# Thresholded attention and a mixer on one core: scores in four quadrants, the up product in 512 columns, quarter-tile down products, the first batch ahead

## The chip, the core and the metric

The kernel runs on one core of a Trainium2 chip. The metric is the device time of one execution in microseconds (us), the median of several runs. The engines are TensorE (PE; its weight loads are listed apart as PEld), VectorE (DVE), ScalarE (ACT), GpSimd (POOL) and SyncE (SP). Each works through its own instructions in the order in which they were written, and waits for other engines by semaphores. DMA is started from SP and POOL here (at the very start from ACT too) and runs on 16 DMA engines that all queues share.

## The reference

There are 8 batches, 8 heads, 576 positions and heads of 64. Attention keeps only the scores within `tau` of a row's maximum; its result, as a 576 x 512 matrix per batch, goes through a mixer of rank 32 along the positions and a hidden layer of 2048.

```python
def _attn_ref(q, k, v, tau) -> np.ndarray:
    scale = 1.0 / np.sqrt(q.shape[-1])
    scores = scale * np.matmul(q, k.transpose(0, 1, 3, 2))
    thresh = np.max(scores, axis=-1, keepdims=True) - tau
    scores = np.where(scores >= thresh, scores, -1000000000.0)
    ...
    attn = np.exp(scores)
    attn = attn / (np.sum(attn, axis=-1, keepdims=True) + 1e-09)
    return np.matmul(attn, v).astype(np.float32)
...
def _moe_ref(x, U, V, w_ch1, w_ch2) -> np.ndarray:
    xt = x.transpose(0, 2, 1)
    h = xt @ U @ V
    u = x + h.transpose(0, 2, 1)
    ch = np.maximum(u @ w_ch1, 0.0) @ w_ch2
    return (u + ch).astype(np.float32)
```

Inputs and output are float32.

## The kernel before

**Tiles.** Heads are taken in pairs: 32 pairs, four per batch. A pair's 576 positions are four tiles of 128 rows and a rest of 64; the rests of two neighbouring pairs share one tile, "tile 4". So two pairs have nine tiles, and the whole kernel 144 score steps, one per tile and pair of heads.

**Attention, per pair.** Twelve DMAs bring q, k and v (`load_tasks`, L268 to L306; the four of v are issued by POOL at L304 and L305). PE transposes q and k in float32 (L334, L349), ACT copies them into `qkT`. A score step (L401 to L414) is a float32 product with a contraction of 64: each head has half of the array's rows, and one matmul makes 128 score rows in 288 columns (L406, four matmuls per step, "two row halves"). Tile 4 uses quadrants of 64 x 64, since its two halves come from two pairs (L411, eight matmuls). In the trace a float32 matmul is two records. Per step and head DVE then scales and takes the row minimum of the negated scores (L427), ACT takes the exponential (L451), and DVE selects and sums (L459) into `w_ring`, a ring of eight bfloat16 tiles. POOL copies the last 64 columns of such a tile a second time (L484), which makes 640. It is then transposed into `wT`: by a DMA transpose from SP (L471; L475 for tile 4), or, for one head of the first eight pairs (`x == 1 and p < EARLY`, 32 tiles), by five PE transposes (L480) and an ACT copy (L494). Values are split into a high and a low bfloat16 part (ACT L371, L372; POOL L376 to L379), and the value product AV (L527, 18 matmuls of 288 columns in "two column halves") runs over both. Its result is transposed back (L554, L557), scaled (L570, L574) and narrowed.

**Mixer.** The rank-32 step is two small PE groups (L592, L607), for tile 4 one more matmul of 512 columns per batch (L610). The sum u is narrowed and transposed (L640, L644 for tile 4) into `uT`, 576 columns per batch. The up product (L682) covers these columns in two halves of 288: 2 x 16 tasks per batch of four matmuls, each followed by a relu on ACT (L692). The down product (L708) makes one tile of 128 rows in two halves of eight matmuls of 512 columns, and holds one PSUM bank for both. Tile 4 holds 64 rows of an even and 64 of the next odd batch. DVE adds u (L721), POOL issues two stores per tile (L734, L735, L738). PSUM has four banks for all of this beside four for the scores.

**The weights** come by POOL's DMAs (L750 to L752, L756 with four casts L759 to L762, eight pieces of W1 at L766, eight of W2 at L769). Each waits in `gate` for the first L427 of a score step.

**The order** is made while the program is built. Every piece is a `Task` with an engine, a cost, a due offset `off` and what it depends on; `Order.run` (L73 to L145) plays them with these costs, and takes on each engine the task that is ready first or, within a small patience, has the lowest rank. Mixer products have a due step (`when`), ahead of which they only fill gaps. Where PE would be idle for over 0.45 us by this plan, it puts in filler matmuls (L234) that compute nothing. The plan's times are not the chip's; only the order that comes of it stays.

## Time and profile before

| | |
|---|---|
| median of 3 runs | 664.34 us (664.3 to 664.85) |
| profiled execution, device time | 662.74 us |
| its span, first to last instruction | 660.9 us |
| mean granted TensorE clock | 0.995 |
| PE busy | 629.7 us (95%) |
| DVE, ACT, POOL busy | 516.4, 492.8, 477.9 us |
| memory read and written | 37.90 and 9.44 MB |

In a group's row stand line, engine, operation, output <- input, shape and count; then busy time, the mean of one in ns, and the engine's idle time ahead of it with what ended it. In rows in order of time stand the start, the duration, and the count of merged records. Matmul records overlap, so what a matmul costs is the distance to the next start and not its duration. Some matmul records are missing (534 of 576 in one group).

### The profile page before, as it was taken

To read this page: it belongs to the slowest core of one execution; us is meant where nothing else is said; L and a number is where in the kernel's file an instruction comes from. 1 tells how busy PE (TensorE), PEld (TensorE's weight loads), DVE (VectorE), ACT (ScalarE), POOL (GpSimd) and SP (SyncE) were. 2 spreads that over 40 slices of the span, in tenths; PEclk is the share of its full clock that TensorE was granted. 3 is DMA by queue.
4 is the path that set the end of the run, shared out by engine and by line. 5 is a ranking of instruction groups with operands and counts; after the bars stand their busy time and mean duration, and the time that the engine had idled before them with its cause. 6 is when DMAs were issued, how large, how long until landed. Compare 5 with 4: busy or idle time off the path is not lost.

```text
span 660.9 us, 15748 instructions
## 1 busy us (share of the span) xinstructions
PE 629.7 (95%) x5121; PEld 409.6 (62%) x5171; DVE 516.4 (78%) x1370; ACT 492.8 (75%) x1122; POOL 477.9 (72%) x864
## 2 busy tenths in 40 slices
PE   8999889999999999999999999999999999999994
PEld 4566556666566666666666666666666666567652
DVE  5999799698798898797997798888995898973001
ACT  4888799888587886778777787868787777776430
POOL 9989788998997779948794889778696965430111
PEclk9999899999999999999999999999999999999998
DMA  4776989999878889869784998976799957561112
GB/s 102 128 112 116 160 121 166 138 153 183 171 152 122 148 148 168 160 101 149 146 159 74 167 170 145 163 130 128 139 184 116 182 122 138 88 108 22 40 41 48
DMA packets 199890, 86.13 MB, mean 130 GB/s; under 512 B 184320, under 2 KB 190416, under 8 KB 199808
## 3 DMA queue, kind: packets, MB, share of 16 engines
q1 hardware_dynamic: 175280, 42.22, 47.1%
q0 software_dynamic: 23648, 42.69, 30.4%
q8 instruction: 41, 0.67, 0.4%
q14 instruction: 41, 0.34, 0.2%
q10 hardware_dynamic: 880, 0.21, 0.1%
HBM read 37.90 MB, written 9.44 MB: 72 GB/s over the span
## 4 chain that ended last, share of the span: by engine, by line
PE 66%; ACT 4%; DVE 3%; issue 2%; POOL 1%; DMA 0%; POOLq 0%; DVEq 0%; ACTq 0%
PE bank L708 18%; PE bank L682 15%; PE scores L406 14%; PE bank L527 9%; PE bank L334 2%; ACT e_sb L451 2%; PE bank L554 2%; PE scores L411 2%; PE bank L592 1%; PE bank L640 1%; ACT R L692 1%; PE bank L607 1%; DVE w_ring L459 1%; DVE s_sb L427 1%; DMA vraw<-in_v_dram 0%
## 5 line engine op out<-in xcount | busy, mean ns | idle before, releaser
L427 DVE TENSOR_SCALAR_CACHE_REDUCE s_sb<-scores 128x576 f32<-128x576 f32 x288 | 206.3, 752 | 63.8 <-PE scores L406 55.2
L451 ACT ACTIVATE e_sb<-s_sb,m 128x576 bf16<-128x576 f32 x288 | 220.4, 768 | 45.4 <-DVE s_sb L427 44.2
L459 DVE SCALAR_TENSOR_TENSOR w_ring<-s_sb,thr,e_sb 128x576 bf16<-128x576 f32 x288 | 232.6, 840 | 6.5 <-issue 4.1
L484 POOL COPY w_ring<-w_ring 128x64 bf16<-128x64 bf16 x288 | 113.4, 407 | 76.3 <-DVE w_ring L459 71.9
L406 PE MATMUL scores<-qkT 64*128 64x288 f32 x1024 | 167.9, 430 | 0.3
L682 PE MATMUL bank<-uT,W1b 128*128 128x288 bf16 x1024 | 138.9, 286 | 2.2 <-ACT R L692 0.9
L708 PE MATMUL bank<-W2b,R 128*128 128x512 bf16 x534 | 129.0, 379 | 4.2 <-issue 1.1
L682 PEld LDWEIGHTS <-W1b 128*128 128x128 bf16 x1024 | 96.1, 98 | 47.2 <-issue 21.5
L692 ACT ACTIVATE R<-bank 128x288 bf16<-128x288 f32 x256 | 94.4, 406 | 40.6 <-PE bank L682 35.7
L406 PEld LDWEIGHTS scores<-qkT 64*128 64x128 f32 x1024 | 95.0, 186 | 43.3 <-issue 11.5
L708 PEld LDWEIGHTS <-R 128*128 128x128 bf16 x576 | 54.5, 98 | 63.9 <-issue 8.5
L288 POOL DMA_DIRECT2D qkraw<-in_q_dram x125 | 82.3, 664 | 16.2 <-PE bank L349 12.3
L288 POOL DMA_DIRECT2D vraw<-in_v_dram x128 | 86.1, 677 | 4.6 <-issue 2.8
L288 POOL DMA_DIRECT2D qkraw<-in_k_dram x125 | 81.5, 657 | 3.2 <-issue 2.4
L527 PE MATMUL bank<-wT,vh 128*64 128x288 bf16 x1152 | 80.4, 290 | 1.6 <-ACT R L692 1.2
L527 PEld LDWEIGHTS <-vh 128*64 128x64 bf16 x1152 | 63.1, 110 | 17.8 <-issue 11.4
L721 DVE TENSOR_TENSOR o<-bank,x 128x512 f32<-128x512 f32 x36 | 24.7, 686 | 45.7 <-PE bank L708 40.3
L734 POOL DMA_DIRECT2D out_dram<-o x32 | 17.9, 561 | 57.1 <-DVE o L721 56.4
L439 ACT ACTIVATE thr<-m,tau_t 128x2 f32<-128x2 f32 x144 | 40.7, 283 | 5.2 <-DVE s_sb L427 5.2
L342 ACT COPY qkT<-bank 128x512 f32<-128x512 f32 x64 | 35.9, 582 | 10.6 <-PE bank L334 10.4
L334 PE MATMUL bank<-ident,qkraw 128*128 128x128 f32 x256 | 37.3, 279 | 4.5 <-DMA qkraw<-in_q_dram 2.6
L377 POOL TENSOR_TENSOR vh<-vraw,vh 128x512 bf16<-128x512 f32 x32 | 38.9, 1216 | 3.5 <-ACT vh L371 0.6
(74 smaller groups left out, 604.8 us busy)
## 6 DMA issues: line engine op xcount, KB each, us to landing
vraw<-in_v_dram POOLq DMA_DIRECT2D x128, 80.0 KB, 3.6
out_dram<-o POOLq DMA_DIRECT2D x72, 128.0 KB, 3.4
qkraw<-in_k_dram POOLq DMA_DIRECT2D x63, 80.0 KB, 4.0
qkraw<-in_q_dram POOLq DMA_DIRECT2D x62, 80.0 KB, 3.7
wT<-w_ring SPq DMA_TRANSPOSE x288, 4.0
qkraw<-in_q_dram POOLq DMA_DIRECT2D x63, 64.0 KB, 3.7
qkraw<-in_k_dram POOLq DMA_DIRECT2D x62, 64.0 KB, 3.6
W1b<-in_moe_w_ch_dram POOLq DMA_DIRECT2D x8, 256.0 KB, 4.7
```

What stands on the lines that cost most here:

```text
L288: queue.dma_start(raw[part, to, j, :], src[:, of, j, :])
L334: nc.tensor.transpose(bank[t.got[0]][:, i * P:(i + 1) * P], pr.qkraw[:, t0 + i, :, :], ident)
L406: nc.tensor.matmul(pair_bank[j][:, c, 0:HC], pr.tT[hs, 0, i * P:(i + 1) * P], pr.tT[hs, 1, c * HC:(c + 1) * HC], start=True, stop=True)
L427: nc.vector.tensor_scalar(out=s_sb.rearrange("p (a c) -> p a c", a=2), in0=pair_bank[x][:, :, 0:HC], scalar1=-scale, scalar2=None, op0=ALU ...
L439: nc.scalar.activation(out=st["thr"], in_=st["m"], func=ACT.Identity, bias=tau_t[:, 0:1], scale=1.0)
L451: nc.scalar.activation(out=st["e", x], in_=st["s", x], func=ACT.Exp, bias=st["m"][:, x:x + 1], scale=-1.0)
L459: nc.vector.scalar_tensor_tensor(out=w_sb[:, 0:S], in0=st["s", x], scalar=st["thr"][:, x:x + 1], in1=st["e", x], op0=ALU.is_le, op1=ALU.mu ...
L484: nc.gpsimd.tensor_copy(out=w_sb[:, S:640], in_=w_sb[:, 512:S])
L527: nc.tensor.matmul(av[64 * j:64 * j + 64, 0:HC], pr.vh[:, kt, part, j, :] if kt < 4 else pr.vh4[:, j, :], pr.wT[:, kt, j, c * HC:(c + 1) * ...
L682: nc.tensor.matmul(bank[t.got[0]][:, 0:HC], W1b[:, dt, ft * P:(ft + 1) * P], bt.uT[:, dt, c * HC:(c + 1) * HC], start=(dt == 0), stop=(dt ...
L692: nc.scalar.activation(out=R2[:, ft, lo:lo + HC], in_=bank[t.got[0]][:, 0:HC], func=ACT.Relu)
L708: nc.tensor.matmul(ch, R2[:, ft, lo:lo + P], W2b[:, ft, :], start=(ft == 0), stop=(ft == 15))
```

## The change

1. *Scores.* Every step uses quadrants: a tile's 128 rows are two halves of 64, so a step is eight matmuls of 64 x 288 where it was four of 128 x 288. The plan's allowance for a change of array mode (`SWITCH`) becomes one per mode.
2. *Up product.* `uT` holds a batch's 512 columns of tiles 0 to 3; one matmul covers 512 columns, 16 tasks per batch and one relu each. Tile 4's 128 columns, of two batches together, get a tile `uT4` of their own, and four tasks per two batches (four hidden tiles of 128 columns side by side in a bank, one relu for the four). Their chain (rank-32 matmul, sum, cast, transposes, copy) is taken out of the last pair's tasks and becomes tasks of its own, at the odd batch.
3. *Down product.* Four tasks of four matmuls per tile, where it was two of eight. Tile 4 comes last.
4. *First batch ahead.* All tasks of pairs 0 to 3 get `off` lower by 20. The loads of v for these pairs (16) are issued by SP. The weights' `off` falls from 25 to 5, V's load and casts are two tasks, and the small ones come first.
5. *Transposes of w.* PE now does 17 tiles: those of `x == 1`, pairs below 8, tiles 2 and 3, and both of pair 3's tile 3. SP's DMA transposes do 15 more.
6. *The plan's DMA times* are kept per queue, with a shared part. Due steps of the mixer move from `18 * (b + 1) + 8` to `+ 12`.

```diff
-    SWITCH = 0.093
-    PARTS = {"S": "two row halves", "S4": "quadrants", "AV": "two column halves"}
+    SWITCH = {"quadrants": 0.145, "two column halves": 0.11, None: 0.095}
+    PARTS = {"S": "quadrants", "AV": "two column halves"}
...
-                if self.PARTS.get(t.kind) != self.PARTS.get(kind):
-                    s += self.SWITCH
+                parts = self.PARTS.get(t.kind)
+                if parts != self.PARTS.get(kind):
+                    s += self.SWITCH[parts]
...
+                q = e != POOL
+                begin = max(moved[q], at[e] + 0.6)
+                shared = min(t.dma, max(0.0, moved[1 - q] - begin))
+                moved[q] = begin + t.dma + shared
+                moved[1 - q] += shared
+                t.end = moved[q] + 1.2
...
-            return add(e, 0.7, fn, deps, dma=0.4, off=20.0 if p else -9.0)
+            return add(e, 0.7, fn, deps, dma=0.2 if e == POOL else 0.35, off=20.0 if p else -9.0)
...
-            loads["v"].append(one("v", POOL, lo, slice(1, 6), slice(0, 5), j, freed))
-            loads["v"].append(one("v", POOL, hi, slice(0, 5), slice(4, 9), j, freed))
+            ev = SP if p < NPAIR else POOL
+            loads["v"].append(one("v", ev, lo, slice(1, 6), slice(0, 5), j, freed))
+            loads["v"].append(one("v", ev, hi, slice(0, 5), slice(4, 9), j, freed))
...
+        now = -20.0 if p < NPAIR else 0.0
         def scores(_):
             for c in range(2):
+                cs = slice(c * HC, (c + 1) * HC)
                 for j in range(2):
                     hs = slice(64 * j, 64 * j + 64)
-                    if i < 4:
-                        nc.tensor.matmul(pair_bank[j][:, c, 0:HC],
-                                         pr.tT[hs, 0, i * P:(i + 1) * P],
-                                         pr.tT[hs, 1, c * HC:(c + 1) * HC], start=True, stop=True)
-                        continue
-                    for a in two:
-                        nc.tensor.matmul(pair_bank[j][a.part4, c, 0:HC], a.tT[hs, 0, 512:S],
-                                         a.tT[hs, 1, c * HC:(c + 1) * HC], start=True, stop=True)
+                    for h in range(2):
+                        a, rows, part = pr, slice(i * P + HB * h, i * P + HB * h + HB), \
+                            slice(HB * h, HB * h + HB)
+                        if i == 4:
+                            a, rows, part = two[h], slice(512, S), two[h].part4
+                        nc.tensor.matmul(pair_bank[j][part, c, 0:HC], a.tT[hs, 0, rows],
+                                         a.tT[hs, 1, cs], start=True, stop=True)
...
-        S_ = done["S", p, i] = add(PE, 0.97, scores, deps, off=-6.0, kind="S" if i < 4 else "S4")
+        S_ = done["S", p, i] = add(PE, 0.97, scores, deps, off=now - 6.0, kind="S", steps=1)
...
-            if x == 1 and p < EARLY and i < 4:
-                t = done["wT", tiles[0]] = add(PE, 0.28, turn_pe, [dup] + free, off=-1.0, banks=1,
+            if i < 4 and (x == 1 and p < EARLY and i >= 2 or p == NPAIR - 1 and i == 3):
+                t = done["wT", tiles[0]] = add(PE, 0.28, turn_pe, [dup] + free, off=now - 1.0, banks=1,
...
+        h = done["h", p] = add(PE, 0.23, spread, [tt, weights0[1]], off=now - 3.0, banks=1, kind="h")
...
+                bt.uT = upool.tile([P, 4, 512], BF16, name="uT", tag="uT")
+            nc.scalar.copy(out=bt.uT[:, pr.hp, :], in_=bank[uT_.got[0]][:, 0:256].bitcast(BF16))
+        done["uT", p] = add(SCA, 0.53, copy_u, [uT_, got("uT", p - 1)], off=now - 2.0, frees=[uT_])
...
+        if not last:
+            return
+        def spread4(t):
+            nc.tensor.matmul(bank[t.got[0]], Vb[:, 512:640], bt.tt, start=True, stop=True)
+        h4 = done["h4", pr.b] = add(PE, 0.22, spread4,
+                                    [done["tt", p - n] for n in range(4)] + [weights0[1]], off=-1.0,
+                                    banks=1, kind="h")
+        def sum_u4(_):
+            nc.vector.tensor_add(out=bt.x4[bt.h4, :], in0=bank[h4.got[0]][bt.h4, :],
+                                 in1=bt.x4[bt.h4, :])
+        u4 = done["u4", pr.b] = add(VEC, 0.62, sum_u4, [h4] + [done["xb", p - n] for n in range(4)],
+                                    off=1.0, frees=[h4])
+        if not bt.odd:
+            return
+        def narrow_u4(_):
+            nc.scalar.copy(out=ub4, in_=bt.x4)
+        ub4_ = add(SCA, 0.57, narrow_u4, [u4, done["u4", pr.b - 1], got("uT4_", pr.b - 2)], off=1.0)
+        def turn4(t):
+            ps = bank[t.got[0]][:, 0:256].bitcast(BF16)
+            for dt in range(4):
+                nc.tensor.transpose(ps[:, dt * P:(dt + 1) * P], ub4[:, dt * P:(dt + 1) * P], identb)
+        uT4_ = done["uT4_", pr.b] = add(PE, 0.23, turn4, [ub4_] + done.get(("p1r", pr.b - 4), []),
+                                        off=-1.0, banks=1, kind="uT")
+        def copy_u4(_):
+            bt.uT4 = upool.tile([P, 4, P], BF16, name="uT4", tag="uT4")
+            nc.scalar.copy(out=bt.uT4, in_=bank[uT4_.got[0]][:, 0:256].bitcast(BF16).rearrange(
+                "p (t c) -> p t c", t=4))
+        done["uT4", pr.b] = add(SCA, 0.53, copy_u4, [uT4_], off=0.0, frees=[uT4_])
...
-        due = 18 * (b + 1) + 8
+        due = 18 * (b + 1) + 12
...
-            for ft in range(16):
-                def up(t, ft=ft, c=c):
-                    for dt in range(4):
-                        nc.tensor.matmul(bank[t.got[0]][:, 0:HC], W1b[:, dt, ft * P:(ft + 1) * P],
-                                         bt.uT[:, dt, c * HC:(c + 1) * HC],
-                                         start=(dt == 0), stop=(dt == 3))
-                t = add(PE, 0.49, up, uT + weights1 + freed, banks=1, kind="p1",
-                        when=due + 9 * c + 9 * ft / 16)
...
+        for ft in range(16):
+            def up(t, ft=ft):
+                for dt in range(4):
+                    nc.tensor.matmul(bank[t.got[0]], W1b[:, dt, ft * P:(ft + 1) * P],
+                                     bt.uT[:, dt, :], start=(dt == 0), stop=(dt == 3))
+            t = add(PE, 0.862, up, uT + weights1 + done.get(("o", b - 2), []), banks=1, kind="p1",
+                    when=due + 9 * ft / 16)
+            done["p1", b].append(t)
+            lo = 640 * bt.odd
+            relus.append(relu_task(t, slice(ft, ft + 1), lo, lo + 512))
+        if bt.odd:
+            done["p1r", b] = []
+            for g in range(4):
+                def rest(t, g=g):
+                    for n in range(4):
+                        ft = 4 * g + n
+                        for dt in range(4):
+                            nc.tensor.matmul(bank[t.got[0]][:, n * P:(n + 1) * P],
+                                             W1b[:, dt, ft * P:(ft + 1) * P], bt.uT4[:, dt, :],
+                                             start=(dt == 0), stop=(dt == 3))
+                t = add(PE, 0.9, rest, [done["uT4", b], got("o4", b - 2)] + weights1, banks=1,
+                        kind="p1", when=due + 9 + 2 * g)
+                done["p1r", b].append(t)
+                relus4.append(relu_task(t, slice(4 * g, 4 * g + 4), 512, 640))
...
-        some = (0, 4) if bt.odd else (0, 1)
-        others = (1, 2, 3) if bt.odd else (2, 3)
-        for i in some + others:
-            near = i in some
+        for i in range(NT if bt.odd else 4):
             halves = []
-            for g in range(2):
+            for g in range(4):
                 def down(t, i=i, g=g, halves=halves):
                     ch = bank[(halves[0] if g else t).got[0]]
-                    lo = 512 if i == 4 else i * P + (S + HB) * bt.odd
-                    for ft in range(8 * g, 8 * g + 8):
+                    lo = 512 if i == 4 else i * P + 640 * bt.odd
+                    for ft in range(4 * g, 4 * g + 4):
                         nc.tensor.matmul(ch, R2[:, ft, lo:lo + P], W2b[:, ft, :],
                                          start=(ft == 0), stop=(ft == 15))
-                deps = relus[0] + ([] if near else relus[1]) + weights2
-                if i == 4:
-                    deps = deps + done["r4", b - 1]
-                when = due + 9 + 9 * ((some.index(i) + g / 2) / 2 if near else
-                                      1 + (others.index(i) + g / 2) / len(others))
-                halves.append(add(PE, 1.73, down, deps + halves, banks=1 - g, kind="ch",
-                                  when=when))
+                when = due + 22 if i == 4 and b < B - 1 else due + 9 + 9 * (i + g / 4) / 4
+                halves.append(add(PE, 0.865, down, (relus4 if i == 4 else relus) + weights2 + halves,
+                                  banks=int(not g), kind="ch", when=when))
...
-            t = gate[n] = add(POOL, cost, fn, [], off=25.0, dma=2.7 if n > 7 else 0.5)
+        def piece(n, fn, cost, to, dma=2.1):
+            t = gate[n] = add(POOL, cost, fn, [], off=5.0, dma=dma)
             to.append(t)
-            n += 2
-        piece(u, 2.1, weights0)
-        piece(vv, 5.0, weights0)
+        piece(2, u, 2.1, weights0, 0.5)
+        piece(1, vv, 0.7, [], 0.5)
+        weights0.append(add(POOL, 2.0, spread_v, [gate[1]], off=5.0))
         for h in range(2):
             for t in range(4):
-                piece(lambda _, t=t, h=h: w1(_, t, h), 1.0, weights1)
+                piece(6 + 2 * (4 * h + t), lambda _, t=t, h=h: w1(_, t, h), 0.7, weights1)
```

On PE, the place where the mixer's first up product stands. `scores` are the score banks, `bank` the other four, `idle` the filler. Before, the rows ahead of the first up product, which follows the 30th score step:

```order
L234 LDWEIGHTS idle
L234 MATMUL bank_151<-idle 128x512
L406 MATMUL scores_148<-qkT 128x288
L406 MATMUL scores_149<-qkT 128x288
L406 MATMUL scores_148<-qkT 128x288
L406 MATMUL scores_149<-qkT 128x288
L682 LDWEIGHTS W1b
L682 MATMUL bank_153<-uT,W1b 128x288
```

Of the change, where it follows the 24th:

```order
L491 LDWEIGHTS w_ring_81
L491 MATMUL bank_152<-identb,w_ring_81 128x128
L421 MATMUL scores_147<-qkT 64x288 x2
L421 MATMUL scores_148<-qkT 64x288 x2
L421 MATMUL scores_147<-qkT 64x288 x2
L421 MATMUL scores_148<-qkT 64x288 x2
L719 LDWEIGHTS W1b
L719 MATMUL bank_150<-uT,W1b 128x512
```

The up product has moved ahead by six score steps, and a step is eight matmuls of 64 rows. The first down product moves from behind the 44th step to behind the 39th.

On POOL, the place of W1's last piece (one row `COPY` is the doubled 64 columns of one of a step's two tiles). Before, behind the 50th copy:

```order
L484 COPY w_ring_80<-w_ring_80 128x64
L484 COPY w_ring_81<-w_ring_81 128x64
L766 DMA W1b<-in_moe_w_ch_dram 128x1024
L288 DMA qkraw<-in_q_dram 64x5x64
L288 DMA qkraw<-in_q_dram 64x4x64
```

Of the change, behind the 39th:

```order
L495 COPY w_ring_86<-w_ring_86 128x64
L295 DMA qkraw<-in_q_dram 64x4x64
L808 DMA W1b<-in_moe_w_ch_dram 128x1024
L295 DMA qkraw<-in_k_dram 64x4x64
L384 CAST v_1307<-vraw 64x128
L385 TENSOR_TENSOR vh<-vraw,vh 128x4x128
```

The last piece has moved ahead by eleven copies, five and a half steps, and no load of v stands between. The last W2 piece goes from behind the 79th copy to behind the 70th.

On SP, the start of the program. Before:

```order
L288 DMA qkraw<-in_q_dram 64x5x64
L288 DMA qkraw<-in_q_dram 64x4x64
L288 DMA qkraw<-in_q_dram 64x5x64
L471 DMA_TRANSPOSE wT<-w_ring_80 128x5x128
L471 DMA_TRANSPOSE wT<-w_ring_82 128x5x128
```

Of the change:

```order
L295 DMA vraw<-in_v_dram 64x5x64 x10
L482 DMA_TRANSPOSE wT<-w_ring_80 128x5x128
L295 DMA vraw<-in_v_dram 64x5x64 x2
L482 DMA_TRANSPOSE wT<-w_ring_81 128x5x128
L482 DMA_TRANSPOSE wT<-w_ring_82 128x5x128
L295 DMA vraw<-in_v_dram 64x5x64 x2
```

The loads of v for pairs 0 to 3 now stand ahead of and between the transposes, and the second head's tile (`w_ring_81`) is transposed here too.

More of the change, by code (lines that the diff above doesn't have):

```diff
@@ L563, in value_tasks @@
                 deps += [got("o4", pr.b - 3)]
-        bk = done["back", p] = add(PE, 0.55, back, deps, off=-3.0, banks=2, kind="back")
+        bk = done["back", p] = add(PE, 0.55, back, deps, off=now - 3.0, banks=2, kind="back")
         def scale_rows(_):
@@ L619, in sum_u @@
                                  in1=bt.x[:, :, pr.cols])
-            if last:
-                nc.vector.tensor_add(out=bt.x4[bt.h4, :], in0=bank[h.got[1]][bt.h4, :],
-                                     in1=bt.x4[bt.h4, :])
-        u = add(VEC, 1.24 if last else 0.62, sum_u, [h], off=-1.5, frees=[h])
+        u = add(VEC, 0.62, sum_u, [h], off=now - 1.5, frees=[h])
         def narrow_u(_):
@@ new lines, in mixer_tasks, with relu_task, relu @@
+        relus, relus4 = [], []
+        def relu_task(t, fts, lo, hi):
+            def relu(_):
+                nc.scalar.activation(
+                    out=R2[:, fts, lo:hi],
+                    in_=bank[t.got[0]].rearrange("p (f c) -> p f c", c=hi - lo), func=ACT.Relu)
+            return add(SCA, 0.5, relu, [t], off=-2.0, frees=[t])
+        done["p1", b] = []
+        for ft in range(16):
[8 more added lines that the diff above has]
+            relus.append(relu_task(t, slice(ft, ft + 1), lo, lo + 512))
```

104 lines of the change are left out of this document (34 added, 70 removed).

## The prediction

> **What bounds the kernel now.** I read the page's busy shares first, then the chain of waits, then a table of four stretches.
>
> ```profile
> PE 629.7 (95%) x5121; PEld 409.6 (62%) x5171; DVE 516.4 (78%) x1370; ACT 492.8 (75%) x1122; POOL 477.9 (72%) x864
> PE 66%; ACT 4%; DVE 3%; issue 2%; POOL 1%; DMA 0%; POOLq 0%; DVEq 0%; ACTq 0%
> 154.42 1.29 PE bank L527 x18
> 180.19 1.22 PE scores L406 x8
> 0.00:110.00 110.00, 99.17 (x782) 62.40 (x789) 95.01 (x268) 85.94 (x179) 97.23 (x181) 0.98 0.79 129
> 110.00:154.00 44.00, 39.77 (x363) 28.22 (x361) 36.20 (x99) 40.02 (x92) 40.48 (x73) 1.00 1.02 148
> 154.00:586.00 432.00, 425.75 (x3512) 277.35 (x3548) 370.00 (x976) 336.18 (x780) 329.06 (x591) 1.00 0.85 144
> 586.00:661.00 75.00, 65.02 (x469) 41.67 (x475) 15.16 (x30) 30.68 (x74) 11.14 (x21) 0.98 0.24 46
> ```
>
> The chain that ended last reaches back to 154 us, three quarters of the span, and 66 of its 77 points are PE: from there the kernel is as long as PE's work. The third stretch says the same: PE 425.8 of 432 us, DVE 370, ACT 336, POOL 329 (columns: PE, PEld, DVE, ACT, POOL, clock, DMA share). Ahead of that PE is not the bound, although it looks busy:
>
> ```profile
> L234 PE MATMUL bank<-idle 128*128 128x512 bf16 x69 | 21.2, 415 | 1.5 <-DVE idle L184 1.2 <-issue 0.2
> 0.00:110.00 110.00, 20.65 (x67) 6.78 (x73) 0.98 0.79 129
> 91.74 0.61 PE L406 MATMUL scores<-qkT 64*128 64x288 f32 x2
> 109.34 1.72 PE L682 MATMUL bank<-uT,W1b 128*128 128x288 bf16 x12
> 110.99 1.37 PE L406 MATMUL scores<-qkT 64*128 64x288 f32 x8
> L766 POOL DMA_DIRECT2D W1b<-in_moe_w_ch_dram x8: 535/576/602, 60.0 to 99.4; - x8
> DMA to landing us min/median/max: 4.1/4.7/6.9
> 167.51 8.58 PE bank L708 x39
> L769 POOL DMA_DIRECT2D W2b<-in_moe_w_ch_dram x8: 716/750/763, 111.0 to 155.1; - x8
> DMA to landing us min/median/max: 4.1/5.1/7.5
> ```
>
> Of the filler matmuls 67 lie in the first 110 us (second row, a table of L234 alone). The first up product starts at 109.3 us, between score steps 30 and 31, and the first down product at 167.5 us. Both follow their weights: the last piece of W1 is issued at 99.4 us and takes 4.1 to 6.9 us, the last of W2 at 155.1 us and 4.1 to 7.5 us. Until then PE has only attention work, while POOL (97.2 of 110 us) and DVE (95.0) set the pace. So there are two questions: how much PE work goes, and how much sooner mixer work can fill the head.
>
> **The change, PE's work.** Prices are distances between starts, since records overlap.
>
> ```profile
> 102.08 1.24 PE L406 MATMUL scores<-qkT 64*128 64x288 f32 x8
> 103.25 0.40 PE L640 MATMUL bank<-identb,ub 128*128 128x128 bf16 x4
> 122.63 1.20 PE L411 MATMUL scores<-qkT 64*64 64x288 f32 x16
> 123.76 0.45 PE L480 MATMUL bank<-identb,w_ring 128*128 128x128 bf16 x5
> 301.12 2.13 PE L682 MATMUL bank<-uT,W1b 128*128 128x288 bf16 x16
> 303.09 0.39 PE L607 MATMUL bank<-tt,Vb 128*128 128x128 bf16 x4
> 117.56 0.44 PE L592 MATMUL bank<-xb_ring,Ub 128*128 128x128 bf16 x5
> 117.84 0.61 PE L334 MATMUL bank<-ident,qkraw 128*128 128x128 f32 x4
> 85.85 0.44 PE L480 MATMUL bank<-identb,w_ring 128*128 128x128 bf16 x5
> 86.22 1.20 PE L411 MATMUL scores<-qkT 64*64 64x288 f32 x16
> 641.66 10.52 PE L708 MATMUL bank<-W2b,R 128*128 128x512 bf16 x47
> ```
>
> *Quadrants.* A step in two row halves takes 103.25 - 102.08 = 1.17 us until the next work can start, and tile 4's step, which already runs in quadrants, 123.76 - 122.63 = 1.13. The change turns 128 steps into that form: 128 x 0.04 = 5.1 us. The twice as many records (16 for 8) are in the 1.13 already. Bounds: rounding of the rows allows 0.02 to 0.06, so 2.6 to 7.7; nothing, if both halves of one tile disturb each other as the two tiles of L411 don't.
>
> *Up product.* At 288 columns one matmul costs 1.97 / 16 = 0.123 us, 1024 of them 126.0. At 512 columns it costs 0.2157 (47 intervals in 10.52 us, less the last record's 0.38), at 128 columns 0.28 / 5 = 0.056. New: 512 x 0.2157 + 256 x 0.056 = 110.4 + 14.3 = 124.8. A gain of 1.2 us only; the columns are the same. What is uncertain is 0.056 in rows of 16 to 64: each matmul there needs a weight load of its own,
>
> ```profile
> L682 PEld LDWEIGHTS <-W1b 128*128 128x128 bf16 x1024 | 96.1, 98 | 47.2 <-issue 21.5 <-DVE w_ring L459 0.4
> ```
>
> and if the loads of 98 ns stopped overlapping, the 256 would cost 256 x (0.098 - 0.056) = 10.8 us more. I take 0.056, since L592 also loads new weights for each of its matmuls; the far end goes to the range. [...]
>
> *Down product* in quarters and tile 4 in steps of its own: the same 576 matmuls, no mode changed, cost nothing on PE. Of tile 4's transposes 16 go (32 to 16): 0.9 us. Tile 4's sum, cast and copies are off PE, under its 425.8 busy us.
>
> *Transposes of w.* 160 matmuls of L480 become 85: 75 x 0.056 = 4.2 us, with 15 ACT copies; 15 tiles go to SP's DMA transposes instead. All lie in the head.
>
> Together 5.1 + 1.2 + 0.9 + 4.2 = 11.4 us. The share behind the start of the 46th step (180.19 us, quoted above) is 88 x 0.04 + 1.0 + 0.9 = 5.4 us, and it lies on the path, as no engine but PE ends a wait there. ACT, which frees PE's banks, does not get in the way:
>
> ```profile
> L692 ACT ACTIVATE R<-bank 128x288 bf16<-128x288 f32 x256 | 94.4, 406 | 40.6 <-PE bank L682 35.7
> L342 ACT COPY qkT<-bank 128x512 f32<-128x512 f32 x64 | 35.9, 582 | 10.6 <-PE bank L334 10.4
> L494 ACT COPY wT<-bank 128x640 bf16<-128x640 bf16 x32 | 21.4, 691 | 0.5 <-PE bank L480 0.4
> ```
>
> A relu over 512 columns should take what L342 takes, 0.58 us against 0.86 us of matmuls; 144 of them are 84 us against 94.4, and 15 copies of 0.69 us go: some 20 us less on ACT.
>
> **The change, the head.** The order above shows the first up product ahead of the 25th step, no longer ahead of the 31st, and the last W1 piece behind 39 copies of POOL instead of 50. Up to the start of step 46 I count instructions by the order and multiply by the prices. Old: 24.3 us of mixer work. New: 23.3 us of it (all 64 up matmuls of 512 columns, 44 down), and 1.8 us more of the remaining work, apart from the transposes that go. So the new kernel has then 5.4 + 0.8 less ahead of it; some more changes of array mode (AV ends 49 times alone, before 45) take 0.7 back: 5.5 us.
>
> When does step 46 start? Old: steps 31 to 45 take 180.19 - 110.99 = 69.2 us, with 61 us of PE work by the same count, 88%. New: step 25 starts at 91.7 us as before, if nothing moves; POOL's prefetching of weights stands ahead of it, which I put at 3 us, so 95. From there to step 46 PE has 70 us of work (23.3 mixer; 21 steps at 1.13, with 0.09 for the change of array mode ahead of each, which is what L480's five take longer ahead of L411, 0.37, than L592's five ahead of L334, 0.28; 21 of the rest). At 88 to 92% that is 76 to 80 us: 171 to 175, I take 173. That is 7.2 us sooner. Bounds: 168 if only the 70 us count and step 25 starts somewhat later, 180 if nothing is won. What supports it on POOL:
>
> ```profile
> L288 POOL DMA_DIRECT2D vraw<-in_v_dram x128 | 86.1, 677 | 4.6 <-issue 2.8 <-POOL vh L379 1.5 <-ACT e_sb L451 0.3
> ```
>
> 16 loads of v leave POOL for SP: 16 x 0.68 = 10.8 us. Counted by the order with the page's mean durations, POOL's work between the copies of steps 31 and 46 falls from 67.6 to 49.5 us; the old figure nearly equals the 69.2 us that these steps took.
>
> On SP the loads stand ahead of and between transposes. Ten come before the first transpose; two of these, of the third pair, need its buffer, which POOL's subtraction for the first pair frees, and POOL does that ahead of the first copy that the transpose awaits. So nothing queues for long behind them. The DMA engines pay:
>
> ```profile
> q1 hardware_dynamic: 175280, 42.22, 47.1%
> wT<-w_ring SPq DMA_TRANSPOSE x288, 4.0
> ```
>
> 47.1% of 660.9 us for 288 transposes, 64 of them of half size, is 311 / 256 = 1.22 us of all 16 engines for a whole one; 15 more are 18.2 us. Up to 110 us the share is 0.79, which leaves 23 us; from 110 to 154 us it is 1.02.
>
> Sum: 662.74 us (the profiled execution: 660.9 of span and 1.8 around it) - 5.5 - 7.2 = 650.0. The median shown is 1.6 higher, 664.34, and would become 651.6: **652 us**. The 6.3 us of the long stretch in which PE is not busy I leave as they are, and the end too (the last sum, two stores).
>
> **Rivals.**
> *The head gives nothing* (step 46 at 180 us, because DVE, 95 of 110 us, already sets the pace): 664.3 - 5.5 = 659. For it: DVE's work hardly changes. Against: PE had no up product at all ahead of 109.3 us, so it can be filled earlier at the same pace of steps.
> *Small matmuls at the pace of their weight loads*: 651.6 + 10.8 = 662. Against: L592, five in 0.28 us. [...]
> *Slower: the DMA engines are the bound in the head.* The eight moved transposes of pairs 4 to 7 fall, with the W2 pieces, where the share is 1.02: 8 x 1.22 = 9.7 us by which wT comes late, and with it AV, batch 1's mixer and PE. Step 46 then starts at 190 us: 664.3 - 5.5 + 9.7 = 668.5. It decides from a delay of 5.5 us on. For it: that share. Against: packets of two queues lie over each other in that figure, so 1.0 need not be full; and the v loads only change queues.
> *Quadrants gain nothing* in steps of one tile: 3.5 us less gain behind the cut, 655; it lies in the forecast's range.
> *More*: step 46 at 168 us, and half of the 6.3 us go, as ACT's load falls and quarters leave the plan more choice on PE: 664.3 - 5.5 - 12 - 3 = 644.
>
> **How the numbers follow.** Forecast (647 to 656) 0.53; head gives nothing 0.14; slow small matmuls 0.07; slower by DMA 0.11; more 0.15. The range of 643 to 661 holds the forecast, most of the empty head and most of "more": 0.8. A difference under 0.2% (663.0 to 665.7) can't be told from none. Faster: 0.53 + 0.15 + 0.13 + 0.04 = 0.85; within 0.2%: 0.04; slower 0.11.
>
> **What would show it.** Right: single score steps 1.13 us from start to next start; up matmuls at 0.216 and in tile 4's groups 0.056; first up product near 95 us, first down near 150, step 46 near 173; the chain still PE from about 150 us. Wrong: gaps of PE in front of AV that end with a transpose's landing and a DMA share over 1.1 before 150 us (the slower rival); tile 4's up products over 0.08 each; a step 46 at 180 or later; or a stretch behind it in which PE waits for ACT or for banks that quarters hold longer.

## The result, and the profile after

The changed kernel takes **646.09 us** (median of 4 runs, 644.88 to 648.5) against 664.38 before (median of 4 runs, 664.3 to 664.85): ratio 0.9728, interval 0.9699 to 0.9757, so 18.3 us faster; forecast were 12.7. Its profiled execution took 645.76 us, 17.0 less than that of before. Single executions in which the chip was in a slower state (1.5% or more above the fastest of the same kernel) are left out of all medians below.

The page of the changed kernel: busy shares, the queue of the DMA transposes, relu, score matmuls:

```profile
span 644.0 us, 17057 instructions
PE 620.2 (96%) x5851; PEld 343.7 (53%) x5851; DVE 517.5 (80%) x1369; ACT 466.3 (72%) x987; POOL 466.8 (72%) x848
q1 hardware_dynamic: 190736, 45.99, 51.8%
L709 ACT ACTIVATE R<-bank 128x512 bf16<-128x512 f32 x144 | 78.5, 588 | 24.5 <-PE bank L719 13.6
L421 PE MATMUL scores<-qkT 64*64 64x288 f32 x2304 | 181.2, 415 | 0.8 <-DVE s_sb L437 0.7
```

ACT's busy time fell by 26.5 us (492.8 to 466.3), and a relu takes 0.588 us against 0.86 of matmuls, so it does not hold PE. The queue of SP's transposes (q1) rose from 47.1% to 51.8%; 15 more transposes and the 16 loads of v that SP now issues are both in it.

Rows of PE in order of time, from the changed kernel's timeline and the end of its chain of waits (L421 score step, L719 up, L735 up of tile 4, L752 down, L540 AV):

```profile
94.58 1.02 PE L719 MATMUL bank<-uT,W1b 128*128 128x512 bf16 x4 [0.26 <-ACT qkT L350]
96.67 1.20 PE L421 MATMUL scores<-qkT 64*64 64x288 f32 x16
146.67 1.89 PE L752 MATMUL bank<-W2b,R 128*128 128x512 bf16 x8 [0.17 <-ACT R L709]
173.79 1.20 PE L421 MATMUL scores<-qkT 64*64 64x288 f32 x16
301.79 1.20 PE L421 MATMUL scores<-qkT 64*64 64x288 f32 x16
302.92 0.66 PE L567 MATMUL bank<-ident,xT_ring 128*128 128x128 f32 x4
602.27 13.81 PE bank L719 x64
628.26 0.89 PE bank L735 x16
```

The first up product starts at 94.6 us (before 109.3), the first down product at 146.7 (167.5), step 46 at 173.8 (180.2). A score step takes 302.92 - 301.79 = 1.13 us. An up matmul takes 13.81 / 64 = 0.216, one of tile 4 0.89 / 16 = 0.056, each of these with its own weight load.

Three stretches of the changed kernel (PE, PEld, DVE, ACT, POOL, clock, DMA share), and then the same middle stretch of the kernel before:

```profile
0.00:200.00 200.00, 184.93 (x1802) 102.35 (x1803) 176.42 (x482) 154.36 (x326) 172.98 (x321) 0.99 1.07 160
200.00:560.00 360.00, 358.32 (x3518) 201.40 (x3517) 313.11 (x824) 275.63 (x593) 276.97 (x495) 1.00 0.85 144
560.00:700.00 140.00, 76.92 (x535) 39.99 (x532) 27.95 (x66) 36.33 (x70) 16.82 (x32) 0.98 0.18 35
```

```profile
200.00:560.00 360.00, 354.76 (x2950) 232.32 (x2974) 309.05 (x819) 282.20 (x653) 277.28 (x496) 1.00 0.87 143
```

PE is idle for 1.7 us between 200 and 560 us; before it was 5.2, of which a part is 24 missing matmul records (2950 beside 2974 weight loads). At the end the two kernels differ in POOL's last drain, an instruction that POOL's sequencer (POOLq) shows around and behind the last store. The changed kernel, then the one before (min/median/max in ns):

```profile
L874 POOLq DRAIN  x3: 51/93/4784, 638.4 to 643.7; - x3
```

```profile
L835 POOLq DRAIN  x3: 51/93/6416, 653.7 to 660.6; - x3
```

In the span, 16.9 us shorter, 6.4 lie ahead of step 46 (180.2 to 173.8) and 10.5 behind it (480.7 to 470.2).

### The profile page after: what moved, and what is told of

Same layout as the page of the kernel before. It is cut to its first block, busy times and chain, and to the rows that moved or that the text cites. A ratio compares the mean times of both kernels' runs of the same rounds, so it can differ in the third digit from the quotient of the medians.

```text
span 644.0 us, 17057 instructions
## 1 busy us (share of the span) xinstructions
PE 620.2 (96%) x5851; PEld 343.7 (53%) x5851; DVE 517.5 (80%) x1369; ACT 466.3 (72%) x987; POOL 466.8 (72%) x848
## 3 DMA queue, kind: packets, MB, share of 16 engines
q1 hardware_dynamic: 190736, 45.99, 51.8%
## 5 line engine op out<-in xcount | busy, mean ns | idle before, releaser
L421 PE MATMUL scores<-qkT 64*64 64x288 f32 x2304 | 181.2, 415 | 0.8 <-DVE s_sb L437 0.7
L752 PE MATMUL bank<-W2b,R 128*128 128x512 bf16 x576 | 133.0, 379 | 0.3 <-ACT R L709 0.2
L719 PE MATMUL bank<-uT,W1b 128*128 128x512 bf16 x512 | 119.1, 380 | 0.6 <-ACT qkT L350 0.3
L421 PEld LDWEIGHTS scores<-qkT 64*64 64x64 f32 x2304 | 78.5, 132 | 67.4 <-DVE s_sb L437 15.9
L709 ACT ACTIVATE R<-bank 128x512 bf16<-128x512 f32 x144 | 78.5, 588 | 24.5 <-PE bank L719 13.6
L752 PEld LDWEIGHTS <-R 128*128 128x128 bf16 x576 | 54.0, 98 | 66.5 <-issue 9.6
L540 PE MATMUL bank<-wT,vh 128*64 128x288 bf16 x1152 | 82.2, 292 | 2.8 <-DMA wT<-w_ring 2.4
L719 PEld LDWEIGHTS <-W1b 128*128 128x128 bf16 x512 | 47.2, 98 | 63.6 <-issue 14.0
L295 POOL DMA_DIRECT2D vraw<-in_v_dram x112 | 75.5, 678 | 2.3 <-issue 1.4
L540 PEld LDWEIGHTS <-vh 128*64 128x64 bf16 x1152 | 62.9, 111 | 21.7 <-issue 13.9
```

The source lines that it names most:

```text
L295: queue.dma_start(raw[part, to, j, :], src[:, of, j, :])
L421: nc.tensor.matmul(pair_bank[j][part, c, 0:HC], a.tT[hs, 0, rows], a.tT[hs, 1, cs], start=True, stop=True)
L540: nc.tensor.matmul(av[64 * j:64 * j + 64, 0:HC], pr.vh[:, kt, part, j, :] if kt < 4 else pr.vh4[:, j, :], pr.wT[:, kt, j, c * HC:(c + 1) * ...
L709: nc.scalar.activation(out=R2[:, fts, lo:hi], in_=bank[t.got[0]].rearrange("p (f c) -> p f c", c=hi - lo), func=ACT.Relu)
L719: nc.tensor.matmul(bank[t.got[0]], W1b[:, dt, ft * P:(ft + 1) * P], bt.uT[:, dt, :], start=(dt == 0), stop=(dt == 3))
L752: nc.tensor.matmul(ch, R2[:, ft, lo:lo + P], W2b[:, ft, :], start=(ft == 0), stop=(ft == 15))
```

## The experiments

Intervals are those of the ratio to the kernel before, which ran beside each. `r_after`, the changed kernel once more, shows how far executions of one program lie apart:

> The changed kernel as it is, beside the three below, so that they are compared on one chip. Expected as before: 0.973 of the kernel before.

It took 646.37 us, 0.9742 (0.9698 to 0.9785), with a span of 641.3 in its profile against 644.0. Its step 46 starts at 171.1 us and not at 173.8; from there to the end both take 470.2 us. So 2 to 3 us between two profiles, or between two medians here, are no finding. "Over the changed kernel" means over 646.2, the mean of its two medians.

### Quadrants alone, and taken back

`e1_quad_alone` is the kernel before with quadrants in every step. The plan does not know of it, so the order is the old one.

```diff
-                        nc.tensor.matmul(pair_bank[j][:, c, 0:HC],
-                                         pr.tT[hs, 0, i * P:(i + 1) * P],
-                                         pr.tT[hs, 1, c * HC:(c + 1) * HC], start=True, stop=True)
+                        for h in range(2):
+                            lo = i * P + HB * h
+                            nc.tensor.matmul(pair_bank[j][HB * h:HB * h + HB, c, 0:HC],
+                                             pr.tT[hs, 0, lo:lo + HB],
+                                             pr.tT[hs, 1, c * HC:(c + 1) * HC], start=True, stop=True)
```

> The kernel before with one edit: all score steps in quadrants; the plan's costs and so the order of every engine stay as they were. Theory (PE's work converts one for one where PE is the bound): a step falls from 1.17 to 1.13 us from start to next start; 88 steps behind the 46th give 3.5 us, those ahead of it give nothing or, through the pace, up to 1.6: 659.3 to 660.9 us. Rival (the gain of the change is one of order and not of quadrants): 663 to 665.

Measured: 660.35 us, 0.9937 (0.9905 to 0.9968); step 46 at 179.7.

`e2_row_halves` is the changed kernel with row halves in the single steps, again in an unchanged order.

```diff
-                    for h in range(2):
-                        a, rows, part = pr, slice(i * P + HB * h, i * P + HB * h + HB), \
-                            slice(HB * h, HB * h + HB)
+                    for h in range(2 if i == 4 else 1):
+                        a, rows, part = pr, slice(i * P, i * P + P), slice(0, P)
```

> The changed kernel with one edit: steps of one tile in two row halves again, same plan, same order. Theory: 646.1 + 3.5 to 5.1 = 649.6 to 651.2 us, PE's idle time in the long stretch unchanged. Rival (in the new order the quadrants only make room for other stalls): 646 to 647.

Measured: 651.04 us, 0.9801 (0.975 to 0.9852), 4.8 us over the changed kernel. One of its steps in the timeline, and its middle stretch:

```profile
310.74 1.24 PE L420 MATMUL scores<-qkT 64*128 64x288 f32 x8
311.91 0.29 PE L604 MATMUL bank<-xb_ring,Ub 128*128 128x128 bf16 x2
```

```profile
200.00:560.00 360.00, 358.27 (x2867) 213.99 (x2865) 310.35 (x817) 272.72 (x587) 274.96 (x493) 1.00 0.85 143
```

1.17 us for the step (311.91 - 310.74), and 1.7 us of idle as with quadrants. So quadrants give 4 to 5 us, at the price per step read from tile 4, and they are not what removed idle time from the long stretch.

### The down product in halves

`e4_down_halves` has two down tasks per tile again.

```diff
-            for g in range(4):
+            for g in range(2):
...
-                    for ft in range(4 * g, 4 * g + 4):
+                    for ft in range(8 * g, 8 * g + 8):
...
-                when = due + 22 if i == 4 and b < B - 1 else due + 9 + 9 * (i + g / 4) / 4
-                halves.append(add(PE, 0.865, down, (relus4 if i == 4 else relus) + weights2 + halves,
+                when = due + 22 if i == 4 and b < B - 1 else due + 9 + 9 * (i + g / 2) / 4
+                halves.append(add(PE, 1.73, down, (relus4 if i == 4 else relus) + weights2 + halves,
```

> The changed kernel with down products in two tasks of eight matmuls again. PE's work is the same. Theory A (quarters let the plan fill PE's gaps: PE not busy in the long stretch fell from 6.3 us to about 2): 646.1 + 2 to 4 = 648 to 650 us, with PE's idle time back. Theory B (fewer ACT instructions and a plan with truer costs closed the gaps): 645.5 to 647.

Measured: 650.9 us, with single executions from 647 to 655; 0.9792 (0.9728 to 0.9856), an interval that reaches from 646 to 655 us and decides nothing. Its profile (span 647.3) has 5.1 us of idle PE between 200 and 560 us, and these waits of PE from 180 to 560 us:

```profile
PE bank L540 <- DMA wT<-w_ring: 3.7, 3, 2.5
PE bank L540 <- ACT R L709: 1.4, 1, 1.4
```

Sporadic: a value product waits three times for a DMA transpose. Whether quarters are the reason that the changed kernel has only 0.9 us of it is not settled.

### The head undone, and parts of it

`e3_head_undone` takes back the lead of the first batch, SP's loads of v, the weights' `off` and PE's part of the transposes.

```diff
-            ev = SP if p < NPAIR else POOL
+            ev = POOL
...
-        now = -20.0 if p < NPAIR else 0.0
+        now = 0.0
...
-            if i < 4 and (x == 1 and p < EARLY and i >= 2 or p == NPAIR - 1 and i == 3):
+            if x == 1 and p < EARLY and i < 4:
...
-            t = gate[n] = add(POOL, cost, fn, [], off=5.0, dma=dma)
+            t = gate[n] = add(POOL, cost, fn, [], off=25.0, dma=dma)
```

> The changed kernel with the head as before: no lead of pairs 0 to 3, their v loads on POOL, weights with the old offset, 32 transposes of w on PE. Scores, mixer and down products stay changed. By the order the first up product stands behind step 31 again, the first down behind step 41. Theory (the head gave the 6.4 us by which step 46 starts sooner): 646.1 + 5 to 7 = 651 to 653 us, step 46 near 179 us. Rival (step 46 comes sooner because of less PE work ahead of it, whatever the head's order): 646 to 648.

Measured: 655.86 us, 0.986 (0.9813 to 0.9908), more than expected: 9.6 over the changed kernel. Step 46 is back at 179.6 us, as expected. The rest lies behind it, 475.6 us where the changed kernel takes 470.2: in it are 2.6 us of waits for DMA transposes, and POOL's drain is back at

```profile
L874 POOLq DRAIN  x3: 51/98/6576, 647.8 to 654.9; - x3
```

`e8_no_lead` takes only the lead back, in `score_tasks` and `value_tasks`.

```diff
-        now = -20.0 if p < NPAIR else 0.0
+        now = 0.0
```

> The changed kernel without the lead of pairs 0 to 3 alone (offset 0 in place of -20); v loads on SP, early weights and transposes stay. By the order the first up product stands behind step 30, no longer 24. Theory (the lead is what lets mixer work start sooner): 4 to 7 us more than the changed kernel. Rival (the weights' earlier landing and the v loads are what counts): at most 2 us more.

Measured: 653.05 us, 0.9808 (0.9754 to 0.9862), 6.8 us over the changed kernel, within the theory's 4 to 7. Its executions scatter from 646 to 656 us and the interval reaches from 648 to 655, so the rival's 2 us are left only at its edge. Step 46 is at 179.3. Rows of its timeline (PE):

```profile
49.74 2.37 PE L540 MATMUL bank<-wT,vh 128*64 128x288 bf16 x18 [1.36 <-DMA wT<-w_ring]
52.04 0.71 PE L605 MATMUL bank<-xb_ring,Ub 128*128 128x128 bf16 x5
56.47 2.32 PE L540 MATMUL bank<-wT,vh 128*64 128x288 bf16 x18 [3.71 <-DMA wT<-w_ring]
58.72 1.79 PE L421 MATMUL scores<-qkT 64*64 64x288 f32 x16
```

PE waits for transposes (1.4 and 3.7 us), and the value product behind such a wait takes 2.3 us instead of 1.2.

`e5_wt_on_pe` gives PE the old 32 tiles of w to transpose.

```diff
-            if i < 4 and (x == 1 and p < EARLY and i >= 2 or p == NPAIR - 1 and i == 3):
+            if x == 1 and p < EARLY and i < 4:
```

> The changed kernel with PE's transposes of w as before the change (32 tiles of the first eight pairs instead of 17; 15 DMA transposes less). Theory A (the 15 moved transposes load the DMA engines in the head, whose share is 1.2 between 40 and 80 us, and PE's waits there for k and wT come from it; PE has idle time there anyway): 2 to 4 us less than the changed kernel. Theory B (taking the 4.2 us of transposes off PE pays): 2 to 4 us more.

Measured: 647.88 us, 0.9753 (0.9715 to 0.9791). Neither: no difference that can be told. Step 46 starts sooner (169.7) although the same 64 up and 44 down matmuls and 75 transposes more stand ahead of it; what is missing there are one value product and 30 of the 76 fillers. The profiled execution, the slowest of its six, loses that again behind step 46: up to 560 us PE waits 3.4 us for transposes and 1.3 us for ACT.

### The figures of the plan

`e7_old_plan`, `e7b_old_plan` and `e7d_old_dma` keep the changed kernel's instructions and put old figures into the plan. `e7_old_plan`:

```diff
-                    s += self.SWITCH[parts]
+                    s += 0.093
...
-                q = e != POOL
-                begin = max(moved[q], at[e] + 0.6)
-                shared = min(t.dma, max(0.0, moved[1 - q] - begin))
-                moved[q] = begin + t.dma + shared
-                moved[1 - q] += shared
-                t.end = moved[q] + 1.2
+                moved[0] = max(moved[0], at[e] + 0.6) + t.dma
+                t.end = moved[0] + 1.2
...
-            return add(e, 0.7, fn, deps, dma=0.2 if e == POOL else 0.35, off=20.0 if p else -9.0)
+            return add(e, 0.7, fn, deps, dma=0.4, off=20.0 if p else -9.0)
...
-        def piece(n, fn, cost, to, dma=2.1):
+        def piece(n, fn, cost, to, dma=2.7):
```

> The changed kernel with the plan's old figures for changes of array mode (0.093 for all) and its old account of DMA (one queue, 0.4 and 2.7 us); what is computed is the same and only the order moves: more fillers (129 for 78), first down product behind step 41. Theory A (the truer plan closed PE's gaps in the long stretch, 6.3 to some 2 us): 2 to 4 us more, in the long stretch. Theory B (it does not matter): within 1 us.

Measured: 663.81 us, 0.9969 (0.9934 to 1.0004). Nearly the whole gain is gone, against both theories (4 us at most). In this order tile 4's row sums are copied for one pair before the first head's part is in. `e7b_old_plan` adds the dependency; in its order pair 8's reciprocal still comes before one part of its row sum. The amount of work is the same in both.

```diff
+        sels = []
...
+            sels.append(sel)
...
-            done["den4", p + 1] = add(SP, 0.6, sums, [sel, got("rec", p - 3)], dma=0.1)
+            done["den4", p + 1] = add(SP, 0.6, sums, [sel, got("rec", p - 3)] + sels, dma=0.1)
```

> All of the change but two of the figures with which the order is planned: the old allowance for a change of array mode (0.093 us for every mode) and the old account of the transfers (one queue for all, 0.4 us a load, 2.7 us a weight piece). The same instructions, in another order; by the order the first up product follows step 25 (24 in the change), the first down product step 41 (39), and 128 filler matmuls stand in it (78). Theory, that these figures belong to what makes the head short: 10 to 17 us over the changed kernel (646), so 656 to 663, step 46 at 185 us or later, and behind 200 us the same pace. Rival, that the figures only rearrange what is bound elsewhere: within 2 us of the changed kernel, 644 to 648, step 46 at 171 to 175 us.

Measured: 654.5 us, 0.9861 (0.9832 to 0.9889), below the theory's 656 to 663 by 1.5 us and 8.3 over the changed kernel; step 46 at 180.2, not at 185. One more dependency in the plan redraws the order and moves the time by 9.3 us.

`e7d_old_dma` is `e7b_old_plan` with the change's allowances for the array mode:

```diff
-                    s += 0.093
+                    s += self.SWITCH[parts]
```

> As e7b_old_plan, but with the change's allowances for a change of array mode, so that only the old account of the transfers is left (119 filler matmuls; first up product behind step 25, first down product behind step 41). Theory, that the account of the transfers is what counts: at most 3 us better than e7b_old_plan. Rival, that the allowance for the array mode counts: half or more of the loss of e7b_old_plan is back.

Measured: 652.87 us, 0.9842 (0.9813 to 0.9872), 1.6 us better than `e7b_old_plan`, as the theory had it and within the scatter; 6.6 us over the changed kernel. The added dependency is in this kernel too, and no run has it alone in the changed kernel, so how much of the 6.6 us is the account of the transfers is not shown. Filler matmuls in the first 200 us, of the changed kernel and of this one:

```profile
L243 PE MATMUL bank<-idle 128*128 128x512 bf16 x76 | 21.3, 410 | 1.2 <-DVE idle L193 1.2
```

```profile
L239 PE MATMUL bank<-idle 128*128 128x512 bf16 x117 | 32.2, 404 | 1.2 <-DVE idle L189 1.2
```

41 more, each 0.2157 us: 8.8 us in which PE computes nothing. By 200 us the changed kernel has started 100 up matmuls against 88 here, and 377 matmuls of value products against 339 (counted by their weight loads).

### A later landing in the plan

`e9_lag` lets the plan expect a transfer 1 us later; `e10_lag_wt` adds `e5_wt_on_pe`'s edit.

```diff
-                t.end = moved[q] + 1.2
+                t.end = moved[q] + 2.2
```

> The change, with the plan's time from the end of a transfer to its use raised from 1.2 to 2.2 us, so that the order puts the products of a transposed tile later (first up product behind step 25, first down product behind step 39, 74 filler matmuls). Theory, that the sporadic waits of value products for their transposes cost the changed kernel some us: 1 to 3 us under the changed kernel, 643 to 645, and waits of PE for wT of under 1 us behind 200 us. Rival, that the waits are cheap or come back elsewhere: 645 to 648.

Measured: 649.22 us, 0.9789 (0.9752 to 0.9825): above both expectations, at best equal to the changed kernel. Between 200 and 560 us PE is busy for 359.7 of 360 us and no longer waits for a transpose, as meant. In the head a wait came back, again with slow work behind it (timeline of PE, then two short stretches):

```profile
52.44 2.37 PE L540 MATMUL bank<-wT,vh 128*64 128x288 bf16 x18 [4.29 <-DMA wT<-w_ring]
54.74 0.61 PE L620 MATMUL bank<-tt,Vb 128*128 128x128 bf16 x4
...
56.41 1.29 PE L540 MATMUL bank<-wT,vh 128*64 128x288 bf16 x18
57.63 0.45 PE L491 MATMUL bank<-identb,w_ring 128*128 128x128 bf16 x5
```

```profile
52.00:54.00 2.00, 1.56 (x14) 1.42 (x16) 1.57 (x4) 0.00 (x0) 0.69 (x1) 0.50 1.06 148
56.00:58.00 2.00, 2.00 (x32) 1.30 (x25) 1.49 (x5) 0.63 (x1) 0.91 (x2) 1.00 1.11 182
```

> e9_lag and 32 tiles of w transposed by PE as before the change (17 in the change), so 15 fewer DMA transposes in the head and 75 more matmuls of 0.056 us; first up product behind step 23, 66 filler matmuls. Theory, that the DMA engines of the head (mean share up to 1.3) hold it back once the order allows for the landing: step 46 at 168 to 171 us and 2 to 4 us under the changed kernel, 642 to 644. Rival, that PE's 4.2 us more of work eat it: 645 to 649.

Measured: 647.3 us, 0.9743 (0.971 to 0.9775), as the changed kernel and in the rival's range. The head's DMA share is lower (0.96 against 1.15 from 40 to 180 us) and PE no longer waits for a transfer between 20 and 180 us. Where that gain goes is not parted: PE has 4.2 us of transposes more, and behind step 46 waits 1.9 us for ACT (row in the last section).

From the profiles (us; fillers are those in the first 200 us, counted by their weight loads, since in some traces their matmul records are incomplete: before, 67 records stand beside 73 loads):

| kernel | step 46 | step 46 to end | first up product | fillers |
|---|---|---|---|---|
| before | 180.2 | 480.7 | 109.3 | 73 |
| quadrants alone | 179.7 | 478.6 | 109.2 | 73 |
| changed, two profiles | 173.8, 171.1 | 470.2, 470.2 | 94.6, 92.2 | 76, 76 |
| row halves again | 173.7 | 473.5 | 93.7 | 76 |
| down in halves | 174.9 | 472.4 | 94.0 | 76 |
| head undone | 179.6 | 475.6 | 115.8 | 63 |
| no lead | 179.3 | 474.5 | 115.6 | 72 |
| w on PE | 169.7 | 479.2 | 91.0 | 46 |
| old plan, and with the dependency | 191.8, 180.2 | 471.0, 471.0 | 104.0, 96.8 | 128, 127 |
| old account of transfers | 177.3 | 473.4 | 95.4 | 117 |
| later landing, and with w on PE | 174.1, 171.5 | 473.0, 474.4 | 96.1, 91.5 | 73, 65 |

## Why the prediction was right, and what it missed

The forecast, 652 us (647 to 656 for its case), has the sign right, and its range of 643 to 661 holds the time. It is 5.5 us too high.

*Quadrants.* 1.17 to 1.13 us a step, 5.1 us in all: measured 1.13, and by `e1` and `e2` 3.9 and 4.8 us. Shown, in unchanged orders.

*Up product.* Priced at 0.2157 and 0.056, measured 0.216 and 0.056. The rival at the pace of weight loads (98 ns) falls: 16 matmuls in a row, each with new weights, keep 56 ns.

*The head.* Forecast 7.2 us, measured 6.4, and 9.1 in `r_after`: first up product at 94.6 (near 95), first down product at 146.7 (near 150), step 46 at 173.8 (near 173). Step 25 came at 96.7 and in `r_after` at 94.3, on both sides of the 95 that were put in. The direction of the cause is shown: without the whole head the loss is 9.6 us, with step 46 back at 179.6, and without the lead 6.8, the latter from executions that scatter over 10 us. How much belongs to which part is not, since each such edit redraws the order, and the two old-plan orders, 9.3 us apart, show what that alone can do. The support on POOL, 10.8 us of v loads, was not tried alone. "Empty head" (659) falls.

*DMA as the bound of the head.* The mechanism is there, but small: the share between 40 and 180 us is 1.15 (0.93 before), and PE waits for loads of k and once in front of AV for a transpose, at 80.6 us, which is the prediction's sign of being wrong. PE's waits for DMA between 20 and 180 us, of the changed kernel and (last row) before, then the changed kernel's transfers issued between 50 and 75 us:

```profile
PE bank L342 <- DMA qkraw<-in_k_dram: 4.2, 3, 3.2
PE bank L540 <- DMA wT<-w_ring: 1.4, 1, 1.4
PE bank L334 <- DMA qkraw<-in_q_dram: 2.6, 2, 2.2
```

```profile
qkraw<-in_k_dram POOLq DMA_DIRECT2D x4, 80.0 KB, 7.4
wT<-w_ring SPq DMA_TRANSPOSE x13, 7.0
```

They take 7.4 and 7.0 us to land where the medians of the whole run are 4.2 and 4.1, so it is the transfers that are slow there, and not only POOL that issues late. Timeline of the changed kernel, and stretches around the longest wait:

```profile
65.10 0.66 PE L342 MATMUL bank<-ident,qkraw 128*128 128x128 f32 x4
68.95 0.63 PE L342 MATMUL bank<-ident,qkraw 128*128 128x128 f32 x4 [3.20 <-DMA qkraw<-in_k_dram]
69.84 4.07 PE L540 MATMUL bank<-wT,vh 128*64 128x288 bf16 x36
73.84 1.20 PE L421 MATMUL scores<-qkT 64*64 64x288 f32 x16
```

```profile
66.00:68.00 2.00, 0.00 (x0) 0.00 (x0) 2.00 (x7) 0.38 (x1) 1.85 (x4) 1.00 1.11 156
70.00:72.00 2.00, 2.00 (x20) 1.51 (x18) 0.85 (x3) 1.73 (x4) 1.96 (x6) 0.50 1.28 221
72.00:74.00 2.00, 2.00 (x24) 1.47 (x24) 0.80 (x4) 0.62 (x3) 2.00 (x6) 0.67 1.11 178
74.00:76.00 2.00, 2.00 (x29) 1.37 (x26) 0.93 (x3) 1.06 (x3) 1.85 (x4) 1.00 1.52 139
```

This wait costs some 5 us, 3.2 of waiting and 1.6 of slow work (two value products from 69.84 to 73.84, 4.0 us instead of 2.4). The kernel before has a wait of 2.2 us for q with slow work behind it (last section). PE's waits for DMA in the head are 5.6 us, 3.4 in `r_after`, against 2.6 before: 1 to 3 us more where the rival had 9.7, so the sign does not turn. The rival was put at W2's transfers and at AV; most of it came earlier, at k. Fewer DMA transposes (`e5`, `e10`) do not pay.

*Where the 5.5 us are.* The step that failed is "the 6.3 us of the long stretch ... I leave as they are, and the end too". Behind step 46 the span lost 10.5 us, not 5.5:
- 1.6 us: POOL's last drain, 6.4 to 4.8 us, which the prediction did not have.
- About 2 us: idle PE in the long stretch. With complete records it is 3.7 us in the old order with quadrants and 1.7 in the changed kernel (row of `e1` below, and above); part of the prediction's 6.3 us were missing records (3512 beside 3548 weight loads). This is the half of "more" that came true. Its reason is not the quadrants (`e2`). The order can do it: from 200 to 560 us the changed kernel's instructions leave 0.3 us of idle in the order of `e9` and 3.7 in that of `e3`. Whether ACT's lighter load has a share is open.
- 1.3 us are not placed; the count of work ahead of step 46 is no more exact than that.

```profile
200.00:560.00 360.00, 356.27 (x3625) 219.88 (x3625) 310.29 (x825) 283.99 (x658) 275.93 (x496) 1.00 0.89 144
```

Less 0.8 us for the head, by the first profile of the changed kernel. The last 1.3 us are the step from the profiled execution to the median: 1.6 us above it before, 0.3 after.

## What to carry to other kernels

Price an array form that is already in the trace by start to start: three such prices held to 0.001 us a matmul or 0.01 a step. Where a planned order fills a head, its figures for transfers may be worth as much as the work that is saved (6.6 us here together with one dependency, beside 5 for the quadrants), but each edit redraws the order, so compare several drawings, or edits that leave the order alone, before a cause is named. The start of a step is a measure of the head only if the same work stands ahead of it: `e4` has 56 down matmuls there and the changed kernel 44, which is 2.6 us of work.

## What was not expected of the hardware

*Some waits cost more than their length.* Behind the 3.2 us wait of the changed kernel PE's granted clock reads 0.50 for 3.4 us (from 69.9 us on, rows from 70.00 to 74.00 above), and in `e9_lag` for 6.8 us (from 48.4 us on, partly inside its wait of 4.3 us; row 52.00:54.00). At that clock 18 matmuls of a value product took 2.3 us instead of 1.22, and a score step of `e8` read 1.79 instead of 1.20 (clock 0.51 from 58 to 60 us). The length of the wait alone does not tell when this happens: in `e10_lag_wt` the clock read 0.50 behind a wait of 1.9 us, and in `e7_old_plan` it read 1.00 from 20 to 60 us, with a wait of 3.3 us in it. What decides it is not shown. Rows of these two kernels, with the stretch behind the first:

```profile
186.50 5.52 PE L719 MATMUL bank<-uT,W1b 128*128 128x512 bf16 x16 [1.86 <-ACT uT L652]
188.00:190.00 2.00, 2.00 (x6) 0.67 (x5) 1.94 (x6) 1.52 (x4) 2.00 (x5) 0.50 0.57 121
38.52 1.26 PE L536 MATMUL bank<-wT,vh 128*64 128x288 bf16 x17 [3.27 <-DMA wT<-w_ring]
```

The prediction had no such price, but it does not part the two kernels: the one before has one stretch of half clock in the head too, also of 3.4 us, behind its wait for q.

```profile
76.74 0.85 PE L334 MATMUL bank<-ident,qkraw 128*128 128x128 f32 x4 [2.19 <-DMA qkraw<-in_q_dram]
78.00:80.00 2.00, 2.00 (x18) 1.24 (x16) 0.00 (x0) 0.23 (x1) 1.33 (x3) 0.50 1.11 140
```

*POOL's last drain* lasted 6.4 to 6.6 us in the three kernels in which POOL issues all loads of v (before, `e1`, `e3`) and 4.6 to 4.9 in all the others. `e8` and `e5` take back the lead and the transposes and keep 4.8 and 4.6, so of the four edits of `e3` the loads of v on POOL and the weights' offset remain. That it is the number of POOL's transfers (470 in those three kernels, 454 in all the others) fits, but was not tested.
